# One written order for the first two feed-forward steps, two state copies on VectorE, and the projection-free step moved from 6 to 4

## The chip, the cores and the metric

The kernel runs on one core of one Trainium2 chip. The metric is device time in microseconds (us) of one execution; lower is better. TensorE (PE) multiplies matrices into PSUM, VectorE (DVE), ScalarE (ACT) and GpSimd (POOL) work elementwise, and SyncE (SP) issues nearly all loads. Each engine works through its own queue in order and waits on semaphores of the others.

## The reference

All tensors are float32. An attention with a decaying state is followed by a feed-forward layer on its output:

```python
# r, k, v: (4, 8, 768, 48); w, u: (8, 48)
for t in range(S):
    cur = np.einsum('bhd,bhe->bhde', u[None] * kt, vt)
    y[:, :, t] = np.einsum('bhd,bhde->bhe', rt, state + cur)
    state = w[None, :, :, None] * state + np.einsum('bhd,bhe->bhde', kt, vt)
x = y.transpose(0, 2, 1, 3).reshape(3072, 384)
h = x @ w_in                                      # w_in: (384, 2048)
g = np.where(h > 0, h, np.exp(np.minimum(h, 0)) - 1)
out = g @ w_out                                   # w_out: (2048, 384)
```

## The kernel before, in words

**Units and chunks.** The 768 time steps are six chunks n of 128, and each chunk has four batches b. A *unit* (n, b) is the attention of 128 steps and 8 heads: r and k are turned (`turn_in`, L616), decayed (`decay_r`, `decay_k`, L676, giving the tile rk), multiplied to scores (`scores`, ps_a, L750), masked (L676 in chunk 0, L831 later), and the outputs are formed (`outputs`, ps_y), which end in the products that the unit adds to its batch's state (`added_state`, L907). For the first chunk the state is only that sum, so `new_state` copies it out of PSUM (two copies a unit, one for each half of the partitions, L924). Later units add it on VectorE to the decayed state (L922).

**Layers.** For each chunk, x (512 rows) goes through 16 steps f, each with 128 of the 2048 hidden columns. A step multiplies x by w_in (`hidden`, L1014, ps_h), applies the activation (`negative`: Relu L1023 and Exp L1024 on ScalarE; `elu`: L1029 on VectorE), and splits the result g into a high part (`split_g` 0, ScalarE, L1035) and a low part (`split_g` 1, VectorE, L1037). `project` (L1058) multiplies both by w_out and sums over f in three banks ps_acc. Every float32 product is made of three products with high and low parts of both sides: nine matrix products of 512 columns for a `hidden`, nine for a `project`. The `project` at a step is that of the step before or, later, of two steps before; `EARLY` says from which step on it is two. At the step where that changes there is no projection.

**Weights.** They are loaded as they are needed, in chunk 0 only: load j = 2f is w_in of step f (four transfers, L215), j = 2f + 1 is w_out of step f (one transfer, L218). Six slots of the tile stage take them in turn, so a load waits until the slot's last reader is done. The weights of pair k (w_out of step k - 1 and w_in of step k) are then widened by ScalarE (`widen`, wide, L559), merged by VectorE (`merge`, L568), their high parts are cast by GpSimd for w_out (`split_w` 0, L579) and ScalarE for w_in (`split_w` 1, L581), and their low parts are what remains (`rest_w`: w_out on GpSimd, L603, w_in on VectorE, L605).

**What sets the order.** The order is written out by hand in strings of short names. `START` holds the four units of chunk 0 and the first weights; `ZERO` is step 0 of chunk 0, `FIRST` the steps 1 to 15, `LATER` the steps of the other chunks. In START and in steps the names are: Lw:j a weight load, Ln:b the three loads (r, k, v) of unit (1, b), H:0 the first half of the columns of layer 0's `hidden`, Y:b the outputs of unit (0, b), xh and xl the high and low part of x, S:b `new_state`, krd:b k times the reversed powers on VectorE (`key_rest`, L722, needed for the added state), flip the reversal of the powers (L536, L537), jk a product that only keeps TensorE busy, wd widen, ma merge, sp split_w, rsd and rs rest_w on VectorE or as described above. The units of chunk 1 begin at the steps in `BEGIN` (2, 5, 8, 11): at such a step a unit is turned, one step later its scores are formed, and one more step later its outputs.

In the kernel before, added states of unit 0 stand in START, those of unit 1 at step 1 and those of units 2 and 3 at step 2 (`last_states`), each followed by its copy on ScalarE. PSUM has three banks for the work outside the layers (tag rw); a bank comes free when its last reader is done.

Of the kernel before, what the change touches and what calls it, by code (L numbers as in the profile page):

```python
# [20 lines left out]
B, H, S, D = 4, 8, 768, 48  # L21
# [4 lines left out]
NF = DFF // P  # L26
NCH = S // P
# [9 lines left out]
EARLY = (0, 6)  # L37
# [6 lines left out]
sum:1 sum:2 vd:1 vd:2 jk:1 Y:0 xh:0 m0:1 m1:1 Tr:3 Tk:3 A:2 xl:0 ru:3 dr:3 dk:3 m0a:2 jk:1 Y:1 m1:2 wd:0 A:3 xh:1  # L44
ma:0 sum:3 xl:1 sp:0 wdi:1 vd:3 m0:3 m1:3 Y:2 flip rsd:0 Lw:6 xh:2 xl:2 mai:1 spi:1 krd:0 jk:1 Y:3 H:0 xh:3 xl:3 S:0 Ln:0
rsd:2 wdo:1 mao:1 spo:1 krd:1 wd:2 rsd:1
"""
ZERO = "Lq hid neg elu kd2 gh gl ma sp kd3 r4d r3 wd"
FIRST = """
hid S Lq rk3 v3 Eq1 ns3 A1 T0 rud0 ma sum0 bkA-1 neg df0 elu sp dk0 pa1 brA-1 Y2 gh gl dr0 pb1 r4d xh2 xl2 mbT+1 mrT+1  # L50
proj krd1 swd2 Dp0 r3 rudx rudA-2 sumA-1 wd third tT+0
"""
LATER = """
# [10 lines left out]
class Kernel:  # L64
# [238 lines left out]
    def run(self):  # L303
        self.start()
        for n in range(NCH):
            for f in range(NF):
                self.step(n, f)
        for f in (NF - 2, NF - 1):
            self.project(NCH - 1, f)
        self.store(NCH - 1)  # L310

    def start(self):
        nc = self.nc

        t = self.wk.tile([P, 2, X // 2], F32, tag="x", name="raw", bufs=2)
        for b in (2, 3):
# [3 lines left out]
        dve = nc.vector  # L320
# [32 lines left out]
            "S": lambda b: self.new_state(0, b),  # L353
            "wd": lambda b: self.widen(b),
# [11 lines left out]
        }  # L366
        for op in START.split():
            name, _, b = op.partition(":")
            ops[name](int(b or 0))
        self.all_banks = False  # L370

# [4 lines left out]

    def last_states(self, f):
        if f == 1:
            self.new_state(0, 1)
            self.next_loads(1)  # L380
        elif f == 2:
            self.new_state(0, 2)
            self.new_state(0, 3)
# [18 lines left out]
    def step(self, n, f):  # L402
# [59 lines left out]
            "S": lambda: self.last_states(f) if n == 0 else None,  # L462
            "kd2": lambda: self.key_rest(0, 2, nc.vector),
            "kd3": lambda: self.key_rest(0, 3, nc.vector),
# [4 lines left out]
        for op in (LATER if n else FIRST if f else ZERO).split():  # L469
# [443 lines left out]
    def new_state(self, n, b):  # L913
# [5 lines left out]
        for i, rows in enumerate(ROWS):  # L919
            state = self.own_state(b, i)  # L920
            if n > 0:
                nc.vector.tensor_add(state, un["sw"][rows], un["ps"][rows])  # L922
            else:
                nc.scalar.copy(state, un["ps"][rows])  # L924
# [216 lines left out]
```

## Time and profile before

| | |
|---|---|
| median of 3 runs | 507.36 us (507.05 to 508.78) |
| profiled execution | 506.66 us |
| span of its trace (first to last instruction) | 504.9 us |
| busy: PE, DVE, ACT, POOL | 98%, 60%, 48%, 22% of the span |
| granted TensorE clock | 1.00 of full speed |

The span is what the rows below are counted from (0 is its first instruction). A row of the timeline gives the start, the duration, the engine, the line, the operation, the tile written and the tiles read, with a bracket where the engine stood idle before and what released it. "x16" counts instructions; a float32 product of turned r, k, scores or states counts two of them for each product.

### The profile page before, as it was taken

To read this page: it belongs to the slowest core of one execution; us is meant where nothing else is said; L and a number is where in the kernel's file an instruction comes from. 1 tells how busy PE (TensorE), PEld (TensorE's weight loads), DVE (VectorE), ACT (ScalarE), POOL (GpSimd) and SP (SyncE) were. 2 spreads that over 40 slices of the span, in tenths; PEclk is the share of its full clock that TensorE was granted. 3 is DMA by queue.
4 is the path that set the end of the run, shared out by engine and by line. 5 is a ranking of instruction groups with operands and counts; after the bars stand their busy time and mean duration, and the time that the engine had idled before them with its cause. 6 is when DMAs were issued, how large, how long until landed. Compare 5 with 4: busy or idle time off the path is not lost.

```text
span 504.9 us, 12122 instructions
## 1 busy us (share of the span) xinstructions
PE 493.3 (98%) x5013; PEld 405.1 (80%) x5013; DVE 303.0 (60%) x528; ACT 241.9 (48%) x462; POOL 109.3 (22%) x145
## 2 busy tenths in 40 slices
PE   8988999999999999999999999999999999999995
PEld 7866877787888888887888888888878878899995
DVE  6777988975765567666475674565674443343331
ACT  2368667653444435435535445354454354344442
POOL 7623333333123231321321312201011000000000
PEclk9999999999999999999999999999999999999999
DMA  9897767583255523635613526415243000011001
GB/s 139 227 194 210 167 198 181 115 161 101 70 111 147 126 73 67 147 71 108 132 44 88 135 58 127 123 33 117 79 85 103 16 1 1 8 28 24 6 0 68
DMA packets 108453, 49.11 MB, mean 97 GB/s; under 512 B 89442, under 2 KB 104292, under 8 KB 108388
## 3 DMA queue, kind: packets, MB, share of 16 engines
q1 hardware_dynamic: 96292, 43.52, 38.5%
q10 hardware_dynamic: 12096, 4.72, 3.8%
q8 instruction: 41, 0.67, 0.6%
q14 instruction: 24, 0.20, 0.1%
HBM read 35.12 MB, written 13.11 MB: 96 GB/s over the span
## 4 chain that ended last, share of the span: by engine, by line
PE 90%; DMA 4%; ACT 2%; DVE 1%; SPq 1%; issue 0%; DVEq 0%; ACTq 0%
PE ps_acc L1058 39%; PE ps_h L1014 37%; PE ps_a L774 4%; PE ps_y L806 3%; DMA stage<-in_moe_w_in_dram 2%; DMA r_t<-in_r_dram 1%; PE ps_y L794 1%; PE ps_a L750 1%; PE ps_y L907 1%; ACT wide L559 1%; PE ps_y L789 1%; PE ps_rT L616 1%; PE ps_kT L616 1%; DMA rev<-in_u_dram 0%; SPq L215 0%
## 5 line engine op out<-in xcount | busy, mean ns | idle before, releaser
L1014 PE MATMUL ps_h<-x,wh 128*128 128x512 f32 (+1 forms) x582 | 180.2, 391 | 0.0
L1058 PE MATMUL ps_acc<-g,wh 128*128 128x512 f32 x480 | 165.9, 400 | 1.4 <-ACT g L1035 1.4
L1029 DVE SCALAR_TENSOR_TENSOR ps_h<-g,ps_h 128x512 f32<-128x512 f32 x96 | 66.7, 695 | 135.3 <-ACT g L1024 135.2
L1014 PEld LDWEIGHTS ps_h<-x,wh 128*128 128x128 f32 x582 | 108.5, 188 | 22.9 <-issue 0.2
L1023 ACT ACTIVATE g<-ps_h 128x512 f32<-128x512 f32 x96 | 57.4, 598 | 135.0 <-PE ps_h L1014 124.2
L1014 PE MATMUL ps_h<-x,wl 128*128 128x512 f32 (+1 forms) x291 | 113.9, 392 | 0.0
L1058 PEld LDWEIGHTS ps_acc<-g,wh 128*128 128x128 f32 x480 | 90.0, 188 | 23.6 <-issue 2.3
L1058 PE MATMUL ps_acc<-g,wl 128*128 128x512 f32 x240 | 93.6, 390 | 0.0
L1037 DVE SCALAR_TENSOR_TENSOR g<-ps_h,g 128x512 fp32r<-128x512 f32 x96 | 66.3, 691 | 41.0 <-ACT g L1035 36.8
L1035 ACT ACTIVATE g<-ps_h 128x512 fp32r<-128x512 f32 x96 | 57.6, 600 | 69.2 <-DVE ps_h L1029 69.0
L1014 PEld LDWEIGHTS ps_h<-x,wl 128*128 128x128 f32 x291 | 54.6, 188 | 13.0 <-DVE wl L605 0.2
L1024 ACT ACTIVATE g<-g 128x512 f32<-128x512 f32 x96 | 60.7, 632 | 3.0
L824 POOL TENSOR_TENSOR a<-ident,diag 128x512 f32<-128x512 f32 x20 | 20.9, 1046 | 155.3 <-PE ps_y L907 77.7
L1058 PEld LDWEIGHTS ps_acc<-g,wl 128*128 128x128 f32 x240 | 45.1, 188 | 9.0
L664 POOL TENSOR_TENSOR tb<-rk,qw 128x512 f32<-128x512 f32 x16 | 20.8, 1298 | 68.6 <-DMA rk<-blocks 62.7
L1058 PE MATMUL ps_acc<-wh,g 128*128 128x384 f32 x128 | 35.2, 338 | 0.0
L831 DVE COPY_PREDICATED a<-mask,ps_a 128x512 f32<-128x512 int32 x40 | 29.4, 734 | 0.0
L820 ACT ACTIVATE a<-ident,diag 128x128 f32<-128x128 f32 x80 | 25.3, 390 | 0.0
L1058 PEld LDWEIGHTS ps_acc<-wh,g 128*128 128x128 f32 x128 | 23.4, 187 | 1.1 <-issue 0.4
L932 ACT CAST x<-ps_y 128x256 fp32r<-128x256 f32 (+1 forms) x40 | 10.8, 324 | 22.5 <-DVE state L922 21.0
L1058 PE MATMUL ps_acc<-wl,g 128*128 128x384 f32 x64 | 21.6, 337 | 0.0
L579 POOL CAST wh<-stage 128x384 fp32r<-128x384 f32 x16 | 9.1, 568 | 54.8 <-DVE stage L568 54.8
(120 smaller groups left out, 454.5 us busy)
## 6 DMA issues: line engine op xcount, KB each, us to landing
blocks<-tb SPq DMA_DIRECT2D x64, 128.0 KB, 2.3
rk<-blocks SPq DMA_DIRECT2D x16, 512.0 KB, 3.4
stage<-in_moe_w_out_dram SPq DMA_DIRECT2D x16, 383.8 KB, 3.3
stage<-in_moe_w_in_dram SPq DMA_DIRECT2D x64, 95.8 KB, 3.4
out_dram<-stage ACTq DMA_DIRECT2D x80, 48.0 KB, 1.7
r_t<-in_r_dram SPq DMA_DIRECT2D x17, 192.0 KB, 4.3
k_t<-in_k_dram SPq DMA_DIRECT2D x17, 192.0 KB, 5.0
v_t<-in_v_dram SPq DMA_DIRECT2D x17, 192.0 KB, 5.3
```

What stands on the lines that cost most here:

```text
L664: (self.nc.gpsimd if i else self.nc.vector).tensor_mul(dst, src, by)
L774: nc.tensor.matmul(un["pa"][i][keys, a * P : (a + 1) * P], lhsT=un["k"][rows, a, keys], rhs=un["r"][rows, a, :], start=True, stop=True, sk ...
L820: self.nc.scalar.activation(un["a"][i][:, a, :], self.ident, AF.Copy, scale=diag[:, a : a + 1])
L824: self.nc.gpsimd.tensor_mul(un["a"][i], self.ident.unsqueeze(1).to_broadcast([P, HP, P]), diag.unsqueeze(2).to_broadcast([P, HP, P]),)
L831: self.nc.vector.copy_predicated(un["a"][i], self.mask.bitcast(I32).unsqueeze(1).to_broadcast([P, HP, P]), un["pa"][i].rearrange("p (a t) ...
L1014: self.nc.tensor.matmul(ph[:, part], lhsT=a[:, c * P : (c + 1) * P], rhs=x[:, c, part], start=(c == 0 and i == 0), stop=(c == NC - 1 and i ...
L1023: nc.scalar.activation(g, ph, AF.Relu, scale=-1.0)
L1024: nc.scalar.activation(g, g, AF.Exp, scale=-1.0)
L1029: self.nc.vector.scalar_tensor_tensor(ph, g, -1.0, ph, op0=ALU.add, op1=ALU.max)
L1035: nc.scalar.activation(part, g, AF.Copy, scale=W_SCALE)
L1037: nc.vector.scalar_tensor_tensor(part, g, W_SCALE, self.g[n, f][2].bitcast(F32), op0=ALU.mult, op1=ALU.subtract)
L1058: self.nc.tensor.matmul(at, lhsT=lhs, rhs=rhs, start=(f == 0 and i == 0), stop=(f == NF - 1 and i == 2),)
```

## The change

Step 0 of chunk 0 and step 1 get one written order, `BOTH`, in the same manner as START; a number without a colon in it is the step that a layer's operation belongs to. `ZERO` and `last_states` go. The copies of the states of units 0 and 1 go to VectorE (`Sd`); those of units 2 and 3 stay on ScalarE, behind the high part of g of layer 1. All four multiplications krd come early in START, flip comes one unit earlier, and the products that keep TensorE busy move from in front of Y:1 to in front of Y:3. `EARLY` goes from step 6 to step 4.

```diff
-EARLY = (0, 6)
+EARLY = (0, 4)
...
-sum:1 sum:2 vd:1 vd:2 jk:1 Y:0 xh:0 m0:1 m1:1 Tr:3 Tk:3 A:2 xl:0 ru:3 dr:3 dk:3 m0a:2 jk:1 Y:1 m1:2 wd:0 A:3 xh:1
-ma:0 sum:3 xl:1 sp:0 wdi:1 vd:3 m0:3 m1:3 Y:2 flip rsd:0 Lw:6 xh:2 xl:2 mai:1 spi:1 krd:0 jk:1 Y:3 H:0 xh:3 xl:3 S:0 Ln:0
-rsd:2 wdo:1 mao:1 spo:1 krd:1 wd:2 rsd:1
+sum:1 sum:2 vd:1 vd:2 jk:1 Y:0 xh:0 m0:1 m1:1 Tr:3 Tk:3 A:2 xl:0 ru:3 dr:3 dk:3 m0a:2 wd:0 flip Y:1 m1:2 A:3 xh:1
+ma:0 sum:3 xl:1 sp:0 wdi:1 vd:3 m0:3 m1:3 Y:2 rsd:0 Lw:6 krd:0 krd:1 krd:2 xh:2 xl:2 mai:1 spi:1 krd:3 jk:2 Y:3 H:0 xh:3
+xl:3 wdo:1 wd:2 rsd:2 mao:1 spo:1 Sd:0 Ln:0 Sd:1
 """
-ZERO = "Lq hid neg elu kd2 gh gl ma sp kd3 r4d r3 wd"
+BOTH = """
+Lw:8 Ln:1 hid0 neg0 elu0 hid1 gh0 rsd:1 Lw:7 neg1 gl0 ma:2 sp:2 elu1 rsd:4 Lw:10 gh1 gl1 S:2 S:3 proj0 wd:3 ma:3 sp:3
+rsd:6 rs:3 Lw:9 rs:5 wd:4
+"""
...
-hid S Lq rk3 v3 Eq1 ns3 A1 T0 rud0 ma sum0 bkA-1 neg df0 elu sp dk0 pa1 brA-1 Y2 gh gl dr0 pb1 r4d xh2 xl2 mbT+1 mrT+1
+Lq rk3 v3 Eq1 hid ns3 A1 T0 rud0 ma sum0 bkA-1 neg df0 elu sp dk0 pa1 brA-1 Y2 gh gl dr0 pb1 r4d xh2 xl2 mbT+1 mrT+1
...
-        for n in range(NCH):
-            for f in range(NF):
-                self.step(n, f)
+        self.first_steps()
+        for at in range(2, NCH * NF):
+            self.step(*divmod(at, NF))
...
+            "Sd": lambda b: self.new_state(0, b, dve),
...
+    def first_steps(self):
...
+        for op in BOTH.split():
+            if ":" in op:
+                self.do(op)
+            else:
+                layer[op[:-1]](int(op[-1]))
...
-    def new_state(self, n, b):
+    def new_state(self, n, b, eng=None):
...
-                nc.scalar.copy(state, un["ps"][rows])
+                (eng.tensor_copy if eng else nc.scalar.copy)(state, un["ps"][rows])
```

Three places where the queues differ follow; line numbers of the changed kernel are 13 or so higher.

ScalarE, from the last cast of x to the activation of step 2, first before, then changed (wide is `widen`, g with L1023, L1024 and L1035 is the activation of a step, wh2 and wh3 are casts of w_in of steps 2 and 3):

```order
L882 CAST x_351<-ps_y_489 128x3x128
L924 COPY state0_59<-ps_st_530 48x4x48 x2
L559 ACTIVATE wide_185<-stage_184 128x384
L559 ACTIVATE wide_185<-stage_184 128x768
L1023 ACTIVATE g_573<-ps_h_518 128x512
...
L559 ACTIVATE wide_185<-stage_184 128x768
L924 COPY state1_60<-ps_st_599 48x4x48 x2
L1023 ACTIVATE g_627<-ps_h_589 128x512
...
L1035 ACTIVATE g_0_633<-ps_h_589 128x512
L559 ACTIVATE wide_185<-stage_184 128x768
L924 COPY state2_61<-ps_st_665 48x4x48 x2
L924 COPY state3_62<-ps_st_684 48x4x48 x2
L1023 ACTIVATE g_721<-ps_h_655 128x512
```

```order
L895 CAST x_351<-ps_y_491 128x3x128
L572 ACTIVATE wide_185<-stage_184 128x384
L572 ACTIVATE wide_185<-stage_184 128x768
L1036 ACTIVATE g_594<-ps_h_520 128x512
...
L1036 ACTIVATE g_612<-ps_h_598 128x512
...
L1048 ACTIVATE g_0_626<-ps_h_598 128x512
L937 COPY state2_61<-ps_st_630 48x4x48 x2
L937 COPY state3_62<-ps_st_649 48x4x48 x2
L572 ACTIVATE wide_185<-stage_184 128x768
L594 ACTIVATE wh3_133<-stage_184 128x384
L572 ACTIVATE wide_185<-stage_184 128x768
L1036 ACTIVATE g_720<-ps_h_694 128x512
```

The copies of units 0 and 1 have left the queue, those of units 2 and 3 stand behind the high part of g of layer 1, and the widenings of pairs 3 and 4 both follow them.

GpSimd, from the zeroing of state 0 on, before and changed (wh1 to wh4 are casts, wl2 to wl4 the low parts of w_out of steps 1 to 3, which the projections of those steps read):

```order
L579 CAST wh1_129<-stage_184 128x384
L579 CAST wh2_131<-stage_184 128x384
L603 TENSOR_TENSOR wl2_132<-stage_184,wh2_131 128x384
L579 CAST wh3_133<-stage_184 128x384
L603 TENSOR_TENSOR wl3_134<-stage_184,wh3_133 128x384
```

```order
L592 CAST wh1_129<-stage_184 128x384
L592 CAST wh2_131<-stage_184 128x384
L592 CAST wh3_133<-stage_184 128x384
L616 TENSOR_TENSOR wl2_132<-stage_184,wh2_131 128x384
L616 TENSOR_TENSOR wl3_134<-stage_184,wh3_133 128x384
```

The cast of pair 3 (wh3) now stands ahead of the low part of pair 2 (wl2).

SyncE's loads from those of unit (1,0) on, before and changed (w_in loads have four transfers, w_out loads one; before, the order is w_out of step 3, w_in of step 4, and so on):

```order
L172 DMA v_t0_70<-in_v_dram 128x8x48
L218 DMA stage_184<-in_moe_w_out_dram 128x1535
L215 DMA stage_184<-in_moe_w_in_dram 32x3x511 x4
L168 DMA r_t1_71<-in_r_dram 128x8x48
L168 DMA k_t1_72<-in_k_dram 128x8x48
L172 DMA v_t1_73<-in_v_dram 128x8x48
L218 DMA stage_184<-in_moe_w_out_dram 128x1535
L215 DMA stage_184<-in_moe_w_in_dram 32x3x511 x4
```

```order
L175 DMA v_t0_70<-in_v_dram 128x8x48
L218 DMA stage_184<-in_moe_w_in_dram 32x3x511 x4
L171 DMA r_t1_71<-in_r_dram 128x8x48
L171 DMA k_t1_72<-in_k_dram 128x8x48
L175 DMA v_t1_73<-in_v_dram 128x8x48
L221 DMA stage_184<-in_moe_w_out_dram 128x1535
L218 DMA stage_184<-in_moe_w_in_dram 32x3x511 x4
L221 DMA stage_184<-in_moe_w_out_dram 128x1535 x2
```

The w_out load of step 3 has moved from ahead of the w_in load of step 4 to behind the three loads of unit (1,1).

## Rows read from the trace of the kernel before

**Rows 1.** The page: busy time of the engines, and the chain that ended last.
```profile
PE 493.3 (98%) x5013; PEld 405.1 (80%) x5013; DVE 303.0 (60%) x528; ACT 241.9 (48%) x462; POOL 109.3 (22%) x145
...
PE 90%; DMA 4%; ACT 2%; DVE 1%; SPq 1%; issue 0%; DVEq 0%; ACTq 0%
```

**Rows 2.** Waits of PE over the whole span: total us, times, longest.
```profile
PE ps_kT L616 <- ACT state L924: 1.6, 1, 1.6
...
PE ps_acc L1058 <- ACT g L1035: 1.4, 1, 1.4
PE ps_a L750 <- DVE rk L676: 0.9, 2, 0.6
```

**Rows 3.** Timeline of PE: start us, duration us, what; states, first waits, score products.
```profile
30.73 0.55 PE L907 MATMUL ps_st<-v_t,k_t 128*32 128x48 f32 x32
32.66 0.47 PE L1058 MATMUL ps_acc<-g,wh 128*128 128x512 f32 x1 [1.38 <-ACT g L1035]
...
37.23 0.89 PE L907 MATMUL ps_st<-raw 128*32 128x48 f32 x64
...
40.31 0.66 PE L616 MATMUL ps_kT<-ident,k_t 128*128 128x128 f32 x4 [1.60 <-ACT state L924]
...
62.22 1.16 PE L750 MATMUL ps_a<-rk 48*128 48x128 f32 x16 [0.36 <-DVE rk L676]
...
78.21 1.16 PE L750 MATMUL ps_a<-rk 48*128 48x128 f32 x16 [0.58 <-DVE rk L676]
...
94.98 1.16 PE L750 MATMUL ps_a<-rk 48*128 48x128 f32 x16
```

**Rows 4.** The chain in order of time: layer 1's projection and layer 3's product.
```profile
40.96 2.08 PE ps_acc L1058 x9
43.04 2.09 PE ps_h L1014 x9
```

**Rows 5.** Timeline of ACT: high part of g, widening, four state copies.
```profile
38.22 0.60 ACT L1035 ACTIVATE g<-ps_h 128x512 fp32r<-128x512 f32 x1 [0.28 <-DVE ps_h L1029]
38.71 1.05 ACT L559 ACTIVATE wide<-stage 128x768 f16<-128x768 bf16 x1
39.63 1.30 ACT L924 COPY state<-ps_st 48x192 f32<-48x192 f32 x4
```

**Rows 6.** Timeline of DVE: two merges, a pair of state adds, rk's last part.
```profile
28.97 0.56 DVE L568 SCALAR_TENSOR_TENSOR stage<-stage,wide 128x384 int32<-128x384 int32 x1 [1.06 <-ACT wide L559]
...
40.98 0.95 DVE L568 SCALAR_TENSOR_TENSOR stage<-stage,wide 128x768 int32<-128x768 int32 x1
...
57.23 0.71 DVE L922 TENSOR_TENSOR state<-sw,ps_y 48x192 f32<-48x192 f32 x2
...
61.40 0.68 DVE L676 TENSOR_TENSOR rk<-ps_rT,pw 128x512 f32<-128x512 f32 x1
```

**Rows 7.** Timeline of POOL: cast and low part of a w_out.
```profile
37.16 0.56 POOL L579 CAST wh<-stage 128x384 fp32r<-128x384 f32 x1 [0.88 <-DVE stage L568]
37.79 1.02 POOL L603 TENSOR_TENSOR wl<-stage,wh 128x384 fp32r<-128x384 f32 x1
```

**Rows 8.** Timeline of SP's queue: v of unit (1,0), w_in of step 4, w_out of step 4.
```profile
28.06 1.13 SPq L172 DMA_DIRECT2D v_t<-in_v_dram  x1
...
31.43 1.84 SPq L215 DMA_DIRECT2D stage<-in_moe_w_in_dram  x4
...
36.30 0.64 SPq L218 DMA_DIRECT2D stage<-in_moe_w_out_dram  x1
```

**Rows 9.** Tile stage, the transfer issued at 36.30 alone: issue to landing.
```profile
DMA to landing us min/median/max: 6.2/6.2/6.2
```

**Rows 10.** By windows: PE, PEld, DVE, ACT, POOL busy, PEclk, DMA share, GB/s.
```profile
31.00:32.00 1.00, 0.28 (x28) 0.14 (x15) 0.81 (x2) 0.24 (x2) 0.00 (x0) 1.00 0.11 20
```

**Rows 11.** Tile stage, the w_out transfer issued at 31.04 alone: issue to landing.
```profile
DMA to landing us min/median/max: 2.9/2.9/2.9
```

**Rows 12.** Timeline of DVE: the pause before the low part of x of unit 2.
```profile
24.87 0.56 DVE L884 TENSOR_TENSOR x<-ps_y,x 128x384 fp32r<-128x384 f32 x1 [1.75 <-ACT x L882]
```

More of the change, by code (lines that the diff above doesn't have):

```diff
@@ L366, in start, with do @@
         }
+        self.ops = ops
         for op in START.split():
-            name, _, b = op.partition(":")
-            ops[name](int(b or 0))
+            self.do(op)
         self.all_banks = False
+    def do(self, op):
+        name, _, b = op.partition(":")
+        self.ops[name](int(b or 0))
+    def first_steps(self):
+        layer = {
+            "hid": lambda f: self.hidden(0, f, self.rest_of(0, f)),
+            "neg": lambda f: self.negative(0, f),
+            "elu": lambda f: self.elu(0, f),
+            "gh": lambda f: self.split_g(0, f, 0),
+            "gl": lambda f: self.split_g(0, f, 1),
+            "proj": lambda f: self.project(0, f),
+        }
+        for op in BOTH.split():
+            if ":" in op:
+                self.do(op)
+            else:
+                layer[op[:-1]](int(op[-1]))
     def next_loads(self, b):
@@ L375, in next_loads @@
         self.load_v(1, b)
[L377 to L383, printed above, removed]
     def stages(self, n, f):
@@ L461, in step @@
             "out": lambda: self.store_next(),
-            "S": lambda: self.last_states(f) if n == 0 else None,
-            "kd2": lambda: self.key_rest(0, 2, nc.vector),
-            "kd3": lambda: self.key_rest(0, 3, nc.vector),
             "third": lambda: self.third_slot() if (n, f) == (0, 14) else None,
@@ L468, in step @@
         now = n * NF + f
-        for op in (LATER if n else FIRST if f else ZERO).split():
+        for op in (LATER if n else FIRST).split():
             if op in layer:
```

## The prediction

> **What bounds the kernel now.** I read the page first: TensorE is busy for 493.3 of 504.9 us and 90% of the chain that ended last runs through it [rows 1]. So only two things can change the time: microseconds in which TensorE waits, and what it is given to do. The work stays the same here (every matrix product is kept, two are reordered and one projection is put off), so the question is where TensorE waits. The list of its waits answers that: 1.6 us once for a ScalarE copy of a state, 1.4 us once for ScalarE's first half of g, and 0.9 us in two pieces for VectorE's decayed r and k (rk) [rows 2]. Then I placed them on TensorE's timeline: the 1.4 us ends at 32.66 in front of layer 0's projection, the 1.6 us ends at 40.31 in front of unit (1,0)'s k transposes, and the two pieces are in front of score products at 62.22 and 78.21; the third such product, at 94.98, waits for nothing [rows 3]. Last I read ScalarE, VectorE, GpSimd and the load queue between 28 and 62 us, because these decide whether a wait that goes comes back elsewhere.
>
> **The two waits that the change addresses.** *Layer 0.* ScalarE now does neither of the first two state copies. A pair of them is half of 1.30 us, so 0.65 [rows 5]. Before the change one pair stands in its queue right ahead of layer 0's activation. That activation can start about 0.65 earlier, yet the second half of layer 0's product now has one more added state ahead of it on TensorE, half of the 0.89 that two take, some 0.45 [rows 3]. The two together put the activation near 29.3 us and, with 0.60 each for its two passes and for the first half of g [rows 5], and 0.68 for VectorE's step between, taken from its rk product of the same shape [rows 6], g is there at 31.8. TensorE ends layer 1's product at 30.73 + 0.45 = 31.2 and now has the added states of units 2 and 3 to do (0.89, taken away from step 2), so it reaches the projection at 32.05 and finds g ready. It gains 0.6 in time and has 0.85 of work behind it that it used to do later: a lead of 1.5.
>
> *The copies on VectorE.* No row shows VectorE copying such a state. Bounds: above, its add of a state of the same shape out of PSUM, 0.71 a pair [rows 6]; below, ScalarE's 0.65 a pair [rows 5]. Two pairs are 1.3 to 1.4 us, and I take 1.4. They stand behind a merge for layer 1 that began at 28.97 after a pause of 1.06 for ScalarE's widening [rows 6]; that widening comes 0.65 earlier too, so the merge ends at 28.97 + 0.56 - 0.65 = 28.9 and the copies at 30.3, just before the activation's VectorE step at 30.5. They lie in idle time; if that cover is gone, they delay the projection by up to 1.4.
>
> *Unit (1,0)'s k transposes.* They need a PSUM bank that ScalarE's copy of a state gives back. The four copies (1.30) now follow the first half of g of layer 1: its two passes end at 33.0, VectorE's step at 34.1 (after the second half of g, 0.7, and a merge of 0.95 [rows 6]), g at 34.7, the copies at 36.0. TensorE gets to the transposes at 36.3: 32.05 + 2.1 for a projection + 2.1 for a product [rows 4]. No wait: the 1.6 is gone too, and with 0.8 for both transposes TensorE is at layer 1's projection at 37.1, 3.8 before its old 40.96 [rows 4].
>
> **The wait that comes instead: layer 1's projection.** Its second matrix product needs the low part of w_out, which GpSimd subtracts. In the new order GpSimd first does the cast of the next layer's weights, and that waits for VectorE's merge, which waits for ScalarE's widening, which stands behind the four copies. So: copies done at 36.0, widening 1.05, merge 0.95, cast 0.56, subtraction 1.02 [rows 5 to 7]: 39.6. TensorE is there at 37.4 and waits 2.2 us. Layer 3's product begins at 37.1 + 2.1 + 2.2 = 41.4 where it began at 43.04 [rows 4]: 1.6 of the lead is left.
>
> **The loads.** ScalarE's next item is widening layer 4's weights, free to start at 38.5 (merge done at 38.0, then a cast of its own, taken to be as long as GpSimd's 0.56 [rows 7]). It needs w_out of layer 3, and on the queue that load now stands behind the three loads of unit (1,1). Before, four w_in loads began to issue at 31.43, then came the three row loads, and the w_out load in the place that this one now has went out at 36.30 [rows 8] and landed 6.2 us later, at 42.5 [rows 9]. Now that same series may begin when the v load of unit (1,0) has been issued, at 28.06 + 1.13 = 29.2, so 2.2 earlier: landing at 40.3. The queue had run empty before the old series (DMA share 0.11 from 31 to 32 us [rows 10]) and has not now, so I add 0.1 and take 40.4. Bounds: late, 42.5, no shift at all; early, 2.9 us from issue, as for the w_out load that met an empty queue [rows 11], so 34.1 + 2.9 = 37.0, before ScalarE is ready for it. [...]
>
> So the widening runs from 40.4 to 41.5 and the merge behind it starts at 41.5, where it started at 40.98 [rows 6]: 0.5 late, although TensorE is early.
>
> **Step 4 without projection.** From that merge on VectorE's and ScalarE's order is unchanged up to the score product of unit (1,1), and it sets the pace: from the merge at 40.98 to the last operand of that product at 61.40 + 0.68 [rows 6] it is 21.1 us, in which VectorE pauses only for ScalarE, not for TensorE. So the operand comes 0.5 later and the score product moves from 62.22 [rows 3] to 62.7. TensorE would be there at 62.22 - 0.4 (its wait before) - 1.6 (lead) - 2.1 (the projection of step 3, put off behind step 4) = 58.1. It waits 4.6 us in all, a little at the scores and outputs of unit (1,0) and at the k transposes of step 5, most of it, 2 to 3 us, at this product. Here the rest of the lead goes.
>
> Behind it TensorE has one projection more to do. From this score product to the next took 62.22 to 78.21, 15.99, with the step that had no projection inside; the next such stretch, 78.21 to 94.98, has a projection in every step and no wait in it, 16.77 [rows 3]. The new stretch has a projection in every step, and since TensorE is later than before against VectorE, I take it without waits: +0.78. **Sum:** 0.5 + 0.8 = 1.3 us later at the product at 78 us. After it the two kernels do the same in the same order, TensorE waits for nearly nothing, and the 1.3 stays to the end. The profiled execution took 506.66, its span of 504.9 and 1.8 around it, so 508.0 against that one; the median of the runs, 507.36, lies 0.7 above it, and 1.3 on top of that gives, rounded, **508.6**. About 0.3% (1.5 us) is what a measurement of this kernel can tell from no change; 508.6 is inside, by little.
>
> The rest costs nothing: the powers' reversal moves ahead by one unit (TensorE does the same products in this stretch without a gap); VectorE's four products of k with rev move into a pause of 1.75 us that it spent waiting for ScalarE's cast behind that reversal [rows 12]. If the cover is gone, each is at most the 0.68 of an rk product [rows 6] in front of the second half of layer 0's product.
>
> **Rivals.** *The load is in time* (for it: rows 11; against: rows 9). Then the merge starts when VectorE, free of its own merge at 38.0, has waited for the cast (38.5) and done a remainder and the two products of ru, tiles as wide as that of the merge of 0.56 [rows 6], near 40.0: 1.0 before its old time. The sum is 0.8 - 1.0 = -0.2, so 507.2, no change. [...]
> *The load is later still* (slower). Place: widening of layer 4. Price: every microsecond past 40.4 is one at the end, since ScalarE's queue stands behind it. It decides from a landing at 40.6 on (1.5 us in the sum); at the late bound of 42.5 the sum is 3.4, 510.8. For it: the queue is fuller than it was; against: less stands ahead of this load than stood ahead of the one at 36.30.
> *TensorE carries its lead to the end* (faster). It needs VectorE's chain to run ahead with it, which would have to hang on TensorE somewhere between 41 and 62 us. Both waits gone and none new: -3.8, 503.6; with the 2.2 us wait for GpSimd, -1.6, 505.8. Against: in that stretch the releaser is VectorE, not the reverse [rows 2, 3].
>
> **Chances.** Forecast (load between 39.4 and 40.6) 0.38, of which all but a little is within 0.3%; load in time 0.14; load later 0.33; lead carried, and errors of the same sign, 0.15, nearly all of it faster by over 0.3%. So faster 0.14, same 0.49, slower 0.37. The range leaves out the best part of the fast case and the last of the slow one: 505.3 to 510.6. The forecast's own range is 507.5 to 509.0.
>
> **What would show it.** Right: no wait for ScalarE at layer 0's projection nor at unit (1,0)'s k transposes; a wait of about 2.2 us for GpSimd at layer 1's projection; one of 2 to 3 us for VectorE's rk at about 62.7; the four copies on VectorE between 28.4 and 30.5; the widening of layer 4 starting at 40.4 with a DMA as its releaser. Wrong: VectorE's rk at 61 us or before, so that the score product waits less than 1 us (then faster); or projections that wait on GpSimd in later layers too (then slower).

## The result and the profile after

The changed kernel takes 509.94 us (median of 8 runs, 509.41 to 511.57), the kernel before 507.08 (8 runs, 505.91 to 508.78): ratio 1.0062, 95% interval 1.0044 to 1.008, so 2.9 us slower. The forecast was 508.6, with a range of its own of 507.5 to 509.0 and a wide one of 505.3 to 510.6, and slower with a chance of 0.37 (same 0.49); the median lies outside the first range and inside the second. The eight runs form two groups, five at 509.4 to 510.0 (mean granted clock 0.996 to 0.999) and three at 511.1 to 511.6 (0.990 to 0.994). The profiled execution took 511.57, its span 509.8, 4.9 above the span before. Lines of the code have moved by 13 (L750 is now L763).

The page: TensorE's busy time, and the chain that ended last. TensorE is 3.4 us longer busy than in [rows 1] with the same 5013 instructions, so part of the loss is not waiting.

```profile
PE 496.7 (97%) x5013; PEld 407.8 (80%) x5013; DVE 306.6 (60%) x532; ACT 240.5 (47%) x458; POOL 108.6 (21%) x145
...
PE 87%; DMA 3%; SPq 3%; DVE 3%; issue 2%; ACT 1%; DVEq 0%; ACTq 0%
```

Waits of PE (total us, times, longest). Both waits of [rows 2] that the change addresses are gone; three others stand there (and one of 0.6 at the k transposes of step 5).

```profile
PE ps_acc L1071 <- POOL wl L616: 1.9, 1, 1.9
PE ps_a L763 <- DVE rk L689: 1.8, 1, 1.8
...
PE ps_y L920 <- issue: 0.9, 1, 0.9
```

Timeline of PE, to be laid beside [rows 3]: layer 0's projection and unit (1,0)'s k transposes without a wait, layer 1's second projection product behind GpSimd, the score products of units (1,1) and (1,2), and a product that stops on its way at 187 us.

```profile
32.28 0.51 PE L1071 MATMUL ps_acc<-g,wh 128*128 128x512 f32 x1
...
37.15 0.60 PE L629 MATMUL ps_kT<-ident,k_t 128*128 128x128 f32 x4
...
39.92 0.50 PE L1071 MATMUL ps_acc<-g,wl 128*128 128x512 f32 x1 [1.93 <-POOL wl L616]
...
63.37 1.16 PE L763 MATMUL ps_a<-rk 48*128 48x128 f32 x16 [1.83 <-DVE rk L689]
...
81.69 1.16 PE L763 MATMUL ps_a<-rk 48*128 48x128 f32 x16
...
187.49 0.24 PE L920 MATMUL ps_y<-v_t,k_t 128*32 128x48 f32 x2 [0.91 <-issue]
```

Timeline of DVE: the four copies, the merge of pair 3, a remainder (wl) and ru's first product (ru is r times u, then times k), the merge of pair 4, the last rk of unit (1,1). The remainder took 1.37 and the product 1.39.

```profile
28.88 1.45 DVE L937 COPY state<-ps_st 48x192 f32<-48x192 f32 x4
...
37.34 0.96 DVE L581 SCALAR_TENSOR_TENSOR stage<-stage,wide 128x768 int32<-128x768 int32 x1 [1.60 <-ACT wide L572]
38.91 1.37 DVE L618 SCALAR_TENSOR_TENSOR wl<-stage,wh 128x384 fp32r<-128x384 f32 x1 [0.61 <-ACT wh L594]
40.20 1.39 DVE L720 TENSOR_TENSOR ru<-r_t,u_b 128x384 f32<-128x384 f32 x1
...
42.10 0.95 DVE L581 SCALAR_TENSOR_TENSOR stage<-stage,wide 128x768 int32<-128x768 int32 x1
...
62.54 0.68 DVE L689 TENSOR_TENSOR rk<-ps_rT,pw 128x512 f32<-128x512 f32 x1
```

The kernel before: timeline of DVE, a merge and the same remainder and product, then of POOL, a subtraction.

```profile
35.71 1.38 DVE L568 SCALAR_TENSOR_TENSOR stage<-stage,wide 128x768 int32<-128x768 int32 x1 [0.33 <-ACT wide L559]
...
39.45 0.55 DVE L605 SCALAR_TENSOR_TENSOR wl<-stage,wh 128x384 fp32r<-128x384 f32 x1
39.92 0.55 DVE L707 TENSOR_TENSOR ru<-r_t,u_b 128x384 f32<-128x384 f32 x1
```

```profile
35.05 1.22 POOL L603 TENSOR_TENSOR wl<-stage,wh 128x384 fp32r<-128x384 f32 x1
```

So the remainder and the product took 0.55 each where no subtraction stood beside them. And the price of one that does stood in this trace already: the merge at 35.71 began inside GpSimd's subtraction and took 1.38, where the merge at 40.98 took 0.95 [rows 6].

Timeline of POOL in the changed kernel, at the time of the long VectorE steps: the cast, then two subtractions in a row, together 2.32.

```profile
38.36 0.53 POOL L592 CAST wh<-stage 128x384 fp32r<-128x384 f32 x1 [4.04 <-DVE stage L581]
38.85 2.32 POOL L616 TENSOR_TENSOR wl<-stage,wh 128x384 fp32r<-128x384 f32 x2
```

The first of the two, in a window that ends before the second begins:

```profile
38.85 1.01 POOL L616 TENSOR_TENSOR wl<-stage,wh 128x384 fp32r<-128x384 f32 x1
```

The first is as long as one alone (1.02 [rows 7]); the second begins at 39.83 and takes 1.35.

Timeline of ACT: the widening of pair 4.

```profile
39.95 1.10 ACT L572 ACTIVATE wide<-stage 128x768 f16<-128x768 bf16 x1 [1.07 <-DMA stage<-in_moe_w_in_dram]
```

Tile stage, the w_out load issued at 33.73 alone.

```profile
DMA to landing us min/median/max: 6.1/6.1/6.1
```

33.73 + 6.1 is 39.8: this is the load that the widening needs. The row above names a w_in load of the next step, which landed at about the same time; experiment e2, where the widening doesn't wait although that w_in load is issued no earlier, shows that it was the w_out.

By windows (columns as in [rows 10]; PEclk is the granted clock as a share of 2.4 GHz).

```profile
41.00:45.00 4.00, 4.00 (x12) 3.16 (x11) 3.96 (x7) 1.84 (x4) 2.06 (x4) 0.57 0.78 227
...
65.00:69.00 4.00, 4.00 (x12) 3.12 (x11) 3.83 (x7) 2.12 (x4) 1.17 (x2) 0.57 0.68 230
```

TensorE stood still before 39.92 and before 63.37, and behind each the granted clock is for most of 4 us at the lower of its two levels, 1.2 GHz. The kernel before:

```profile
30.00:75.00 45.00, 41.42 (x457) 32.13 (x456) 38.34 (x67) 31.92 (x61) 15.36 (x20) 1.00 0.79 192
```

**Where 4.9 us come from**, along the timeline: the first hidden product begins 0.37 later (26.02 for 25.65; over all the profiles of this case it begins anywhere from 25.3 to 27.0). The merge of pair 4 comes 16.08 behind that start for 15.33: +0.75. The score product of unit (1,1) is thus 1.15 late. The next one is 18.32 behind it for 15.99: +2.33. The pause at 187 us: +0.91. And 0.42 behind the last hidden product, a piece that takes 12.5 to 13.0 us in the profiles of this case. That is 4.8 of the 4.9.

### The profile page after: what moved, and what is told of

Read it like the earlier page. It is cut to its first block, busy times and chain, and to the rows that moved or that the text cites. A ratio compares the mean times of both kernels' runs of the same rounds, so it can differ in the third digit from the quotient of the medians.

```text
span 509.8 us, 12123 instructions
## 1 busy us (share of the span) xinstructions
PE 496.7 (97%) x5013; PEld 407.8 (80%) x5013; DVE 306.6 (60%) x532; ACT 240.5 (47%) x458; POOL 108.6 (21%) x145
## 4 chain that ended last, share of the span: by engine, by line
PE 87%; DMA 3%; SPq 3%; DVE 3%; issue 2%; ACT 1%; DVEq 0%; ACTq 0%
PE ps_acc L1071 39%; PE ps_h L1027 37%; PE ps_a L787 3%; PE ps_y L819 3%; SPq L218 2%; DMA r_t<-in_r_dram 1%; PE ps_y L807 1%; PE ps_y L920 1%; PE ps_y L802 1%; DMA stage<-in_moe_w_in_dram 1%; PE ps_a L763 1%; ACT wide L572 1%; DVE stage L581 1%; DMA raw<-in_v_dram 1%; SPq L171 1%
## 5 line engine op out<-in xcount | busy, mean ns | idle before, releaser
L1050 DVE SCALAR_TENSOR_TENSOR g<-ps_h,g 128x512 fp32r<-128x512 f32 x96 | 66.3, 691 | 40.3 <-ACT g L1048 35.2
```

The source lines that it names most:

```text
L1050: nc.vector.scalar_tensor_tensor(part, g, W_SCALE, self.g[n, f][2].bitcast(F32), op0=ALU.mult, op1=ALU.subtract)
```

## The experiments

In the diffs, a line of an order string is cut to the names around the change. "Stretch" is short for the half-clock stretch at 65 to 69 us; the one at 41 to 45 us is called the first stretch. Times stand as median (lowest to highest; ratio to the kernel before, its 95% interval). A useful measure inside one profile is the distance from the merge of pair 3 to that of pair 4: 42.10 - 37.34 = 4.76 in the changed kernel. From the start of the merge of pair 4 to the start of the last rk of unit (1,1) it is 20.44 in the changed kernel, 20.42 in the kernel before and 20.42 or 20.43 in e1 to e3 and f1: once that merge is placed, VectorE places the score product.

### What holds the merge of pair 4 (e1, e2, f1)

e1: GpSimd's subtraction for layer 1's projection ahead of its cast.
```diff
-ma:2 sp:2 elu1 rsd:4
+ma:2 sp:2 rs:3 elu1 rsd:4
...
-rsd:6 rs:3 Lw:9
+rsd:6 Lw:9
```
Expected: 

> Edit: GpSimd's subtraction for the w_out of layer 1's projection goes in front of the cast that waits for the merge, directly behind the cast of its own w_out; nothing else changes. Theory A (VectorE is held up at 38.9 to 41.6 us by GpSimd's two subtractions, 1.37 and 1.39 us for steps that elsewhere take 0.55, and so the merge of pair 4 begins at 42.10): with only one subtraction left there the merge begins at about 41.1, the last rk of unit (1,1) comes 1.0 us earlier (61.5 for 62.54), the 1.9 us wait at layer 1's projection and the half-clock stretch behind it are gone, and the time falls by about 1.0 us, to 508.9. Theory B (the load of w_out sets the merge, as forecast): the merge stays within 0.3 us of where it is and the time stays at 509.9, though TensorE's wait at the projection goes.

Measured: timeline of DVE in e1, then of ACT.

```profile
36.80 0.96 DVE L581 SCALAR_TENSOR_TENSOR stage<-stage,wide 128x768 int32<-128x768 int32 x1 [1.60 <-ACT wide L572]
38.38 0.56 DVE L618 SCALAR_TENSOR_TENSOR wl<-stage,wh 128x384 fp32r<-128x384 f32 x1 [0.62 <-ACT wh L594]
38.86 1.39 DVE L720 TENSOR_TENSOR ru<-r_t,u_b 128x384 f32<-128x384 f32 x1
...
40.98 0.96 DVE L581 SCALAR_TENSOR_TENSOR stage<-stage,wide 128x768 int32<-128x768 int32 x1
```

```profile
39.86 1.09 ACT L572 ACTIVATE wide<-stage 128x768 f16<-128x768 bf16 x1 [1.51 <-DMA stage<-in_moe_w_in_dram]
```

With one subtraction left only one step of VectorE is long. The distance of the merges falls from 4.76 to 4.18, 0.58 and not the 1.0 of theory A, because the load stops it next: the merge follows the end of the widening (40.95) at once. The last rk begins at 61.40 and the wait at layer 1's projection is gone. The time did not fall: 510.12 (508.85 to 512.28; 1.0072, 1.0052 to 1.0093). TensorE now has a wait of 2.30 at the score product of unit (1,0), and the profile shows half clock behind it (0.71 from 44 to 48 us) as well as behind unit (1,1)'s (0.59 from 62 to 66).

e2: the w_out load ahead of unit (1,1)'s rows.
```diff
-Lw:8 Ln:1 hid0 neg0 elu0 hid1 gh0 rsd:1 Lw:7 neg1
+Lw:8 hid0 neg0 elu0 hid1 gh0 rsd:1 Lw:7 Ln:1 neg1
```
Expected: 

> Edit: the w_out load of step 3 is issued ahead of the three row loads of unit (1,1), as in the kernel before. Both theories: it lands before 37.5 us and the widening of pair 4 begins at about 38.9, without a DMA as releaser, 1.0 earlier than 39.95. Theory A (GpSimd's two subtractions hold VectorE until 41.6): the merge stays at 42.1 and the time at 509.9, within 0.4. Theory B (the load sets the merge): the merge comes 0.6 to 1.0 earlier and the time falls by as much, to 508.9 to 509.3.

Measured: timeline of ACT, of DVE, and of PE in e2.

```profile
39.04 1.05 ACT L572 ACTIVATE wide<-stage 128x768 f16<-128x768 bf16 x1
```

```profile
39.16 1.36 DVE L618 SCALAR_TENSOR_TENSOR wl<-stage,wh 128x384 fp32r<-128x384 f32 x1 [0.62 <-ACT wh L594]
40.45 1.39 DVE L720 TENSOR_TENSOR ru<-r_t,u_b 128x384 f32<-128x384 f32 x1
...
42.35 0.95 DVE L581 SCALAR_TENSOR_TENSOR stage<-stage,wide 128x768 int32<-128x768 int32 x1
```

```profile
63.60 1.16 PE L763 MATMUL ps_a<-rk 48*128 48x128 f32 x16 [1.84 <-DVE rk L689]
80.38 1.16 PE L763 MATMUL ps_a<-rk 48*128 48x128 f32 x16
```

The load is out of the way (issued at 32.39, landed 4.2 later) and the merge doesn't move: the distance is 4.76 again. That is theory A, for this place. The time is 510.98 (509.25 to 512.21; 1.0085, 1.0071 to 1.0099), no gain, and 0.7 above what theory A allowed; four of the six runs have a mean clock of 0.991 or 0.992, like the changed kernel's profile with both stretches, so the rows decide here and not the median. The profiled execution is the one of 509.25: the same two waits, but a granted clock of 1.00 from 30 to 75 us. So such a wait may bring the half clock and need not. Without it the two score products are 16.78 apart, for 15.99 before.

f1: both edits.
```diff
-Lw:8 Ln:1 hid0 neg0 elu0 hid1 gh0 rsd:1 Lw:7 neg1
+Lw:8 hid0 neg0 elu0 hid1 gh0 rsd:1 Lw:7 Ln:1 neg1
...
-ma:2 sp:2 elu1 rsd:4
+ma:2 sp:2 rs:3 elu1 rsd:4
...
-rsd:6 rs:3 Lw:9
+rsd:6 Lw:9
```
Expected: 

> Edit: the two edits before together (GpSimd's subtraction for layer 1's projection ahead of its cast; w_out load of step 3 ahead of unit (1,1)'s rows). Theory (two limits on the merge of pair 4 lie within 1 us of each other: GpSimd against VectorE until 42.1, the load until 41.05, so that either alone hides the other): now the merge begins when VectorE is free, at 40.0 to 40.6, and 20.4 us later, at 60.4 to 61.0, the last rk of unit (1,1). Score product at 61.2 to 61.8 for 63.34. Time without a half-clock stretch behind that product 507.9 to 508.5, with one 509.5 to 510.0; both may occur, since TensorE now waits 2 us or more at the score product of unit (1,0), too. Rival (the projection that stands behind the product is not on the path): faster than the kernel before, 506 or less.

The widening begins at 38.89 without a wait, and the merge at 41.41, a distance of 3.97: 0.79 less than in the changed kernel, where e1 had 0.58 and e2 nothing. It is 0.8 later than the window expected, as VectorE's 1.39 beside the remaining subtraction stays. Two limits, one behind the other, as the theory says, GpSimd's the later one. Time 509.41 (508.58 to 512.34; 1.0047, 1.0026 to 1.0068), about 1 us later than expected without a stretch; its profile has the first stretch (0.60 from 44 to 48 us) and the pause at 185 us, but behind the wait of 1.83 at unit (1,1)'s product the clock is 1.00.

### The projection put off (e3, g2)

e3, in the changed kernel:
```diff
-EARLY = (0, 4)
+EARLY = (0, 6)
```
Expected: 

> Edit: EARLY = (0, 6) again, so that step 6 is the one without projection, not step 4. Theory (one projection more lies behind the score product of unit (1,1), which VectorE sets; and the wait there brings the second half-clock stretch): TensorE does one projection more ahead of that product, reaches it at about 63.6 for 61.5, waits less than 0.3 us, and the stretch at half clock at 65 to 68 us is gone. The time falls by 0.5 against the after-runs without that stretch and by 2.1 against those with it: about 509.2, and the 5 runs lie within 1 us of each other. Rival (the put-off projection costs nothing, it is hidden later): 509.9, no change.

Measured: 508.77 (507.29 to 509.08; 1.0035, 1.0021 to 1.0049). Timeline of PE in e3:

```profile
63.23 1.16 PE L763 MATMUL ps_a<-rk 48*128 48x128 f32 x16 [0.58 <-DVE rk L689]
79.20 1.16 PE L763 MATMUL ps_a<-rk 48*128 48x128 f32 x16 [0.61 <-DVE rk L689]
```

The wait is 0.58 for 1.83 (more than the 0.3 expected), the next product 15.97 later, no half clock behind it. 1.2 us below the changed kernel's median, as the theory has it; the two intervals just overlap, so it is the rows that carry this.

g2, the other way round in the kernel before:
```diff
-EARLY = (0, 6)
+EARLY = (0, 4)
```
Expected: 

> Edit of the kernel before: only EARLY = (0, 4), so that step 4 and not step 6 is without projection. Theory (VectorE sets the score product of unit (1,1), so that a projection put off from ahead of it to behind it is lost time): the last rk stays at 61.4, 20.4 us behind the merge of pair 4, the product at 62.2, TensorE waits there 2.4 us for 0.36, and the next such product comes 16.8 us later for 16.0. Time 0.8 us above the kernel before where the clock holds (508.2 against 507.4), 2.3 above it where the half-clock stretch follows the new wait. Rival (the put-off projection is made up for in a later wait): within 0.3 of the kernel before.

Measured: 508.70 (507.83 to 510.42; 1.0023, 1.0006 to 1.004). Timeline of PE in g2:

```profile
64.44 1.16 PE L750 MATMUL ps_a<-rk 48*128 48x128 f32 x16 [1.85 <-DVE rk L676]
81.19 1.16 PE L750 MATMUL ps_a<-rk 48*128 48x128 f32 x16
```

16.75 between them for 15.99, and a wait that is longer by 1.5. The two places (e3 and g2) give the same: 0.8 us for the one projection that VectorE no longer hides. The time is 1.2 above the kernel before in the same rounds (507.49), for 0.8 expected. The profiled execution here was a late one (509.77): its load of weights for the next pair held the widening by 0.75, and its start was 1.3 later.

### The half clock and the pause at 187 us (e4, g4)

e4: seven products of the identity in front of unit (1,1)'s score product, into a tile of the hidden product's banks.
```diff
         un = self.units[n, b]
+        if (n, b) == (1, 1):
+            self.keep_warm(7)
         un["pa"] = self.products(un["k"], un["r"])
```
Expected: 

> Edit: seven products of the identity with itself (no result is used) stand on TensorE ahead of the score product of unit (1,1), so that it is at work for some 1.3 to 1.5 of the 1.83 us that it waited there. Theory (the half-clock stretch at 65 to 68 us follows from TensorE standing still at that product, and it is what parts runs of 511.1 to 511.6 from those of 509.4 to 510.0): the profile shows the granted clock at 1.00 from 62 to 75 us, the time is 509.4 to 510.0 in every run, none above 510.8. Rival (the clock falls for another reason, such as the load of that part of the program): the stretch stays and runs above 511 stay.

Timeline of PE in e4:

```profile
62.66 1.83 PE L511 MATMUL junk<-ident 128*128 128x128 f32 x14 [1.13 <-DVE g L1052]
64.42 1.16 PE L765 MATMUL ps_a<-rk 48*128 48x128 f32 x16
```

The filling itself waited 1.13 us for a bank and moved the score product 1.05 back: badly placed. Yet the time was not later, 509.38 (508.87 to 510.41; 1.0057, 1.0043 to 1.0071), and none above 510.8: no stretch (1.00 from 62 to 75 us), and the pause at 187 us was gone as well, which no theory had said. Two runs, at 510.4, lie above the 509.4 to 510.0 that was expected of every run.

g4: six products into the bank that the score product overwrites.
```diff
-        un["pa"] = self.products(un["k"], un["r"])
+        un["pa"] = self.products(un["k"], un["r"], 6 if (n, b) == (1, 1) else 0)
...
-    def products(self, kw, rw):
+    def products(self, kw, rw, fill=0):
...
         pa = [self.bank("a") for _ in range(2)]
+        for _ in range(fill):
+            self.nc.tensor.matmul(pa[0][:, 0:P], lhsT=self.ident, rhs=self.ident, start=True, stop=True)
```
Expected: 

> Edit of the changed kernel: six products of the identity with itself into the bank that the score product of unit (1,1) is about to overwrite, ahead of it. They wait for nothing (the seven of the earlier run waited 1.1 us for a bank of the hidden product and moved the score product to 64.4) and fill 1.5 of the 1.83 us. Theory: the score product stays at 63.3 to 63.4, the granted clock stays at 1.00 behind it, and the pause of 0.9 us at about 187 us, which four kernels show at the same instruction and the earlier run with products in front does not, is gone. Time 508.4 to 509.2, 0.9 to 1.5 below the changed kernel. Rival (the clock falls all the same): 509.9 or more in half of the runs.

Timeline of PE, and a window of g4:

```profile
60.83 1.50 PE L761 MATMUL ps_a<-ident 128*128 128x128 f32 x12
62.73 1.16 PE L765 MATMUL ps_a<-rk 48*128 48x128 f32 x16 [0.40 <-DVE rk L689]
```

```profile
63.00:67.00 4.00, 4.00 (x30) 3.33 (x29) 3.37 (x6) 3.56 (x7) 1.57 (x2) 1.00 0.74 207
```

The clock holds behind the product, while the earlier half-clock stretch, behind the projection that was left as it was, is still there (0.57 from 39 to 43 us). 508.12 (507.53 to 510.92; 1.0019, 1.0006 to 1.0032): work that nobody uses, put into a wait, saves 1.8 us, 0.3 more than expected. Of this, 0.9 is the pause. As to the clock, none of the 18 runs of e4 and g4 has a mean clock under 0.993, while 9 of the 20 runs of the changed kernel, e2 and h2 have 0.992 or less. But the median of the changed kernel lies among its runs of 0.996 to 0.999, so what is left of the 1.8, another 0.9, stays open. In g4's profile the score product comes 37.46 behind the first hidden product, in the changed kernel's 37.35: its earlier place in the rows is that of an earlier start, not of the filling.

For the pause, all fourteen profiles can be laid side by side, worked out from their packets of the queue of kind "instruction" (16,384 bytes each): how long before the added-state product a packet of this queue starts, and the longest distance between two instructions of the product (0.09 where it runs through).

| kernels | packet starts before the product | longest distance |
|---|---|---|
| before, e4, f3, f4, g2, g4, h1 | 1.80 to 2.70 us | 0.09 to 0.24 us |
| changed, e1, e2, e3, f1, f2, h2 | 0.84 to 1.38 us | 0.55 to 1.17 us |

The packets take 0.92 to 1.36 us each. No edit was made for this alone, but e4 and g4 differ from the changed kernel, and f3 from f2, by nothing but products of the identity, and have no pause. The table shows that the pause goes with a late packet, and in all seven kernels that have it, it stands in front of the last two of the 32 products. That TensorE stands for its program there is the reading that I take, not a thing shown by itself. The Trainium skill (page "Runtime: NRT & Kernel Launch", section "Instruction fetch mechanics") says that an engine's program is brought in blocks of 16 KiB ahead of use, and that crossing a block is mostly hidden: the size agrees, and "mostly" leaves room for these 0.5 to 1.2 us.

### The copies back on ScalarE (h2)

```diff
-mao:1 spo:1 Sd:0 Ln:0 Sd:1
+mao:1 spo:1 S:0 Ln:0 S:1
```
Expected: 

> Edit of the changed kernel: the four copies that VectorE does go back to ScalarE, in the same place. Theory (on VectorE they are free, on ScalarE they stand ahead of layer 0's activation): the activation begins 0.7 later, TensorE waits 0.5 to 0.7 us for g at layer 0's projection, widening and merges behind it come 0.6 to 0.8 later, and so does everything up to the score product of unit (1,1): time 510.4 to 510.9. Rival (covered by the waits that come later): no change from the changed kernel, 509.9.

Timeline of PE in h2:

```profile
32.84 0.47 PE L1071 MATMUL ps_acc<-g,wh 128*128 128x512 f32 x1 [0.49 <-ACT g L1048]
```

The wait is back, 0.49, and the merge of pair 4 comes at 42.62 for 42.10, with the first hidden product at 26.02 in both. That is the theory, at or just under its lower end. The score product of unit (1,2) is still 0.53 later (82.22 for 81.69). The time doesn't show it: 511.47 (508.91 to 511.81) is 1.5 above the changed kernel's median, but four of the six runs have a mean clock of 0.992 or 0.993, that of a profile with both half-clock stretches, where the changed kernel has two of eight; against the kernel before in the same rounds the ratio is 1.0066 (1.0045 to 1.0086) for 1.0062.

### Towards a faster kernel (f4, f2, f3, h1)

f4: in the kernel before, the last rk ahead of the halves of g.
```diff
-elu sp dk0 pa1 brA-1 Y2 gh gl dr0 pb1
+elu sp dk0 dr0 pa1 brA-1 Y2 gh gl pb1
```
Expected: 

> Edit of the kernel before: only the decayed r (dr0) in front of the halves of g in the later steps of layer pass 0. Theory (in the kernel before VectorE's rk holds the score products of units (1,1) and (1,2), by 0.36 and 0.58 us): the rk comes 0.6 us earlier, both waits are gone, and the time falls by 0.5 to 0.9 us, to 505.8 to 506.2 against 506.7 of the kernel before. Rival (the second half of g, now 0.6 later, holds a projection instead): no change.

506.73 against 507.39 (0.9986, 0.9972 to 0.9999): both waits for rk are gone; 0.7 us, though not beyond what can be told.

f2: f1 with two more edits.
```diff
-EARLY = (0, 4)
+EARLY = (0, 6)
...
-elu sp dk0 pa1 brA-1 Y2 gh gl dr0 pb1
+elu sp dk0 dr0 pa1 brA-1 Y2 gh gl pb1
```
Expected: 

> Edit: the one before, EARLY = (0, 6), and in the order of the later steps of layer pass 0 the decayed r (dr0) in front of the halves of g. Theory (VectorE's chain sets the score product of unit (1,1), the lead is lost there): the last rk comes at 59.8 to 60.4, TensorE with its one projection more is not there before 60.8 to 61.5 and does not wait; no projection more stands behind it. The product begins 0.7 to 1.4 before the 62.19 of the kernel before and the time is 0.7 to 1.4 below it, 505.3 to 506.0; if the half-clock stretch comes (behind the wait of 1 to 2 us at unit (1,0)'s product) it is no longer hidden and the time is 506.5 to 507.5. Rival (the product is held by something else in this stretch): 507.5 or more.

Measured: 507.33 (506.18 to 508.09; 0.9995, 0.9982 to 1.0007). Timeline of PE, and a window of f2:

```profile
62.29 1.16 PE L763 MATMUL ps_a<-rk 48*128 48x128 f32 x16
```

```profile
44.00:48.00 4.00, 4.00 (x22) 3.29 (x23) 2.55 (x4) 3.41 (x8) 1.47 (x3) 0.58 0.70 186
```

The last rk begins at 60.97, over half a us later than expected, and TensorE doesn't wait for it, but arrives only at 62.29: a wait of 2.1 at unit (1,0)'s product, half clock behind it, and the pause of 1.0 later. The time is the one foreseen for that case; whether for the reason foreseen, f3 tells.

f3: six products of the identity into the bank of unit (1,0)'s score product, into f2 by the edit of g4 with another unit.
```diff
...
+        un["pa"] = self.products(un["k"], un["r"], 6 if (n, b) == (1, 0) else 0)
...
```
Expected: 

> Edit: the one before, and six products of the identity with itself into the bank that the score product of unit (1,0) is about to overwrite, ahead of it, so that TensorE is at work for 1.1 us of its wait there (six of 0.13 to 0.19). Theory (the half-clock stretch follows a standstill of TensorE): the granted clock stays at 1.00 from 30 to 75 us in the profile, and the time is 505.3 to 506.2 in most runs, the median below the run without the six. Rival (the clock falls all the same): as that run, or 0.2 to 0.5 later where the six hold up the product.

Timeline of PE in f3:

```profile
41.85 1.50 PE L761 MATMUL ps_a<-ident 128*128 128x128 f32 x12
44.06 1.16 PE L765 MATMUL ps_a<-rk 48*128 48x128 f32 x16 [0.71 <-DVE rk L689]
```

505.95 (505.20 to 507.15; 0.9974, 0.9962 to 0.9985), 1.4 below f2, with the clock at 1.00 from 30 to 75 us. In the two profiles only 0.26 of it is there at the score product of unit (1,1) (62.03 for 62.29) and nothing at that of unit (1,2) (77.97 for 77.88); 1 us appears at 183 us, where f3 has no pause. So in these two profiles the filling gained by moving the program, not by the clock, and what f2 lost was the pause and not, as foreseen, a half clock that is no longer hidden.

h1: f3, and GpSimd's last subtraction there goes to VectorE.
```diff
-Lw:9 rs:5 wd:4
+Lw:9 rsd:5 wd:4
```
Expected: 

> Edit of the run with four edits and six products (f3): GpSimd's remaining subtraction in that place (low part of layer 2's w_out) goes to VectorE. Theory (beside GpSimd's subtraction VectorE's step on two tiles takes 1.39 for 0.56, so VectorE loses 0.83 to spare itself 0.56): the merge of pair 4 comes 0.2 to 0.3 earlier against the first hidden product (15.0 for 15.3 us), and the time is 0 to 0.3 lower, 505.7 to 506.0, below what this can tell. Rival (the 1.39 is no effect of GpSimd): the step stays at 1.39 and the merge comes 0.56 later.

Timeline of DVE in h1:

```profile
37.46 0.96 DVE L581 SCALAR_TENSOR_TENSOR stage<-stage,wide 128x768 int32<-128x768 int32 x1 [1.60 <-ACT wide L572]
39.04 0.56 DVE L618 SCALAR_TENSOR_TENSOR wl<-stage,wh 128x384 fp32r<-128x384 f32 x1 [0.62 <-ACT wh L594]
39.52 0.55 DVE L616 TENSOR_TENSOR wl<-stage,wh 128x384 fp32r<-128x384 f32 x1
39.98 0.55 DVE L720 TENSOR_TENSOR ru<-r_t,u_b 128x384 f32<-128x384 f32 x1
...
41.05 0.95 DVE L581 SCALAR_TENSOR_TENSOR stage<-stage,wide 128x768 int32<-128x768 int32 x1
```

VectorE does one step more and is done earlier: the distance of the merges is 3.59, for 3.96 in f3. (Counted from the first hidden product, as the expectation has it, the merge is not earlier, 15.79: in this profile TensorE began early and stopped for x twice, by 0.32 and 0.21, inside that product.) The 1.39 was GpSimd's doing. Time 505.61 (505.30 to 506.56; 0.9964, 0.9952 to 0.9977), 1.9 us below the kernel before in the same rounds (507.49) and 4.3 below the changed one: the fastest of this study, though not to be told from f3.

## Why the prediction was right, and where it was short

The forecast of 508.6 lies 1.3 below the measured median; the sign and the chain of waits were right. The load landed at 39.8, in the case that the forecast was made for (39.4 to 40.6), and still the median is outside that case's range of 507.5 to 509.0. It falls inside the wide range only because that was stretched for a load later still, which did not come; what filled the gap is not in the forecast. That part is luck. Step by step:

- *The two waits that the change addresses.* Gone, as forecast; layer 0's projection at 32.28 (32.05), the copies 1.45 (1.4) at 28.88 in VectorE's idle time. h2 shows what they would cost on ScalarE, 0.5.
- *The wait that comes instead.* 1.93 for GpSimd until 39.92 (forecast 2.2 until 39.6). That the clock falls behind it was not foreseen: layer 3's product begins at 42.45 for 41.4, of which 0.3 is the wait's later end. It costs nothing at the end, since VectorE is later still: in e2, with the clock at 1.00 there, TensorE waits 0.67 at unit (1,0)'s score product instead, and 1.84 at unit (1,1)'s all the same.
- *The loads.* The w_out load landed 6.1 us after its issue, at 39.8 (40.3), and the widening began at 39.95 (40.4). The row that the prediction went by, 6.2, was the right one: a w_out load on an empty queue took 2.9 [rows 11], one with the four w_in loads in front, in e2, 4.2, and one with these and the three row loads in front 6.1.
- *The merge at 41.5.* This term failed: 42.10. The prediction put the merge down to the load and the widening behind it, and took the remainder and ru's products, of which it spoke only in a rival, at the length of a merge as wide, 0.56 [rows 6], while GpSimd's subtractions now stand beside them, and there such a step takes 1.37 to 1.39. Counted from the first hidden product the merge is 0.75 late where 0.5 was forecast, and for another reason: the widening ended at 41.05 and the merge began 1.05 later, and e2 shows that the load, to which the whole delay was put down, had no part in it. That the size came out near is luck. The trace of the kernel before had the price, in the merge of 1.38 at 35.71.
- *VectorE's chain to the score product.* 21.1 from the merge to the end of the last rk was forecast, 42.10 to 63.22 is 21.1. The product is at 63.37 (62.7), with a wait of 1.83 (2 to 3).
- *One projection more: +0.78.* 16.78 in e2, 16.75 in g2 for 15.99: +0.76 to 0.79. Right.
- *"After it the two kernels do the same".* Here two terms were missing. The half clock behind the score product costs 18.32 - 16.78 = 1.54 in the profiles that have it (e1 and h2 have 18.28 and 18.34 there). The pause of 0.91 at 187 us stands in the profile of the changed kernel and not in that of the kernel before; that the unprofiled runs have it too is not shown.

So, against the kernel before, without the stretch: 0.75 + 0.79 + 0.91 = 2.45, and the five runs at 509.4 to 510.0 are 2.3 to 2.9 above 507.08. The other three, with the lower mean clock, have a median 1.2 above that of the five, where a stretch is 1.54 in the profile.

The rival "the load is in time" fell with its price, 507.2: in e2 the load is in time and the kernel no faster. It had VectorE done with ru near 40.0, which needs GpSimd out of the way. "TensorE carries its lead to the end" fell as argued: VectorE sets unit (1,1)'s product.

## What to carry to other kernels

A wait that is taken from the matrix engine early is worth only what the engine behind it can follow: look for the next place where another engine's unbroken chain ends in something it needs, and don't put off matrix work to behind that place. Steps moved from one engine to another must be priced with what runs beside them there, not with their mean. A wait that is left can be filled with matrix products into a bank that is about to be overwritten, which kept the clock up in the runs of e4 and g4; see in the trace whether the gain is the clock's, or that of a program whose parts now lie elsewhere.

## What the runs showed of the hardware

- VectorE's steps with two operands in SBUF take 1.36 to 1.40 us for 0.55 where they begin inside a subtraction of GpSimd (by 0.05 to 0.45 us after its start), and a subtraction that begins inside such a step takes 1.22 to 1.41 for 1.01 to 1.05; the one that begins first is not longer (1.01 at 38.85; 0.56 for the VectorE step at 38.38 in e1). In h1, without the subtraction, the steps take 0.55. The Trainium skill (page "SBUF — State Buffer", section "Who interferes with whom") says that a VectorE instruction with two SBUF inputs contends with a GpSimd instruction that reads SBUF, the second one being blocked while the first runs. The trace agrees: of two that overlap the later one is longer, and the loss of VectorE, 0.84, is most of one subtraction.
- The granted clock fell to the lower level behind some standstills of TensorE of 1.8 to 2.3 us and not behind others of the same length (e2, f1, g2); the kernel before, with waits of 1.6 and 1.4, shows none in its profile.
- A product of 32 small matrix products stopped for 0.5 to 1.2 us, with nothing to wait for that the profile shows, in seven of the fourteen kernels, depending on what stands ahead of it in the program.
